# Reciprocals of the softmax sums turned by a transposing DMA instead of TensorE, and a pairwise minimum whose subtraction comes first

## The chip, the cores and the metric

The kernel runs on one core of a Trainium2 chip. The core has TensorE (PE; its weight loads are listed apart as PEld), VectorE (DVE), ScalarE (ACT) and GpSimd (POOL); each executes its own queue of instructions in order and waits at semaphores. SyncE (SP) issues nearly all of this kernel's DMAs, in order as well. SBUF is the on-chip memory, PSUM holds what PE writes, DRAM is off the core. The metric is the device time of one execution in microseconds (us), the median of some runs.

## The reference

```python
# q, k, v: (B, H, S, D) = (8, 8, 576, 64); w_in: (512, 2048); w_out: (2048, 512); all float32
scores = (1 / sqrt(D)) * q @ k.T                  # per batch and head, 576 x 576
kth = 32nd largest of each row
scores = where(scores >= kth, scores, -1e9)
attn = exp(scores - max(scores))
attn = attn / (sum(attn) + 1e-9)
x = (attn @ v) with heads side by side            # (4608, 512)
h = x @ w_in
out = (h * 1 / (1 + exp(-1.702 * h))) @ w_out     # (4608, 512)
```

## The kernel before, in words

**Slots.** Attention is cut into 144 slots. A slot is a batch, a tile of 128 query rows and a pair of heads; the last 64 rows of a batch are put together by two head pairs. A batch has 18 slots. The order of the work on each engine is written out by hand. Slots 0 to 12 are done one by one in an opening, in which the weights are loaded too. From slot 13 on a loop, `two_slots` (lines 852 to 942), handles two slots at a time, 68 passes in all. What follows is this loop; a pass is called a period.

**Scores and search.** PE multiplies q and k (line 283), ACT copies the 128 x 2 x 576 scores to SBUF (line 295). To find the 32nd largest of a row, DVE works on pairs of scores: `pair_up` (lines 319 to 328) writes the larger of each pair, `greater` (line 324, DVE), and the smaller, `lesser`. GpSimd makes the latter in 32-bit integer arithmetic on the bit patterns as a + b - max(a, b): the addition is line 327, the subtraction line 328. `topk_of_pairs` (lines 330 to 371) is a list of 23 DVE steps: fourteen MAX8 and MATCH_REPLACE8 on `greater` (numbers 0 to 13), then `pair_up` for the next slot (14), then six on `lesser` (15 to 20), and two reductions (21 and 22), the last of which writes `cut` (line 357). The function `find` (lines 868 to 874) executes the list and hangs other work between its steps.

**Softmax.** `lows` (line 378, GpSimd) makes a bias from `cut`; ACT pushes down what is below the cut (line 398), exponentiates and sums the rows (line 401). The sums of two slots stand together in `sums`, 128 x 4. `split` (line 471, ACT) puts the high and the low 16-bit halves of the exponentials apart and a DMA writes them to DRAM as `rows` (line 473); a transposing DMA, which handles 2-byte elements, reads them back turned, as `pt` (line 479).

**Values and x.** One period later PE multiplies `pt` and v into the PSUM tile `o` (`values_at`, line 539); the columns of `o` are query rows. Each is to be divided by its row's sum, which lies along partitions in `sums`. So `invert` (lines 425 to 437) adds 1e-9 (line 430) and takes reciprocals (line 432) on DVE, and GpSimd copies each to 64 columns (`wide`, line 434). It is called after step 8 of the odd slot's search, for the two slots of the period before. `sum_rows` (line 528) turns `wide` on PE against the identity matrix, twice a period, into the other half of `o`. Then ACT copies all of `o` to SBUF (`x`, line 924) and GpSimd multiplies the one half by the other (`x_of`, line 553) into `xT`. `finish_x` hands on an `xT` whose four head pairs are complete.

**Hidden layer.** `hidden` (line 587) multiplies `xT` and `w_in` in quarters, two quarters a period; ACT takes tanh (line 604) and copies (607), GpSimd forms the gated value (616, 617), PE multiplies by `w_out` (`project`, line 635), and ACT and a DMA take the result out (641, 643).

**Queues.** On PE a period is: a quarter of `hidden`, `project`, `sum_rows`, scores, values, scores, the second quarter of `hidden`, `project`. On GpSimd it is: lows and gate, lines 434 and 327 and 328, lows and gate, `x_of`, lines 327 and 328. SP issues: fetches of q and k in some periods (lines 185, 188), rows of the first slot, q and k split in halves in other periods (245 to 250), the transposing DMA of the first slot, of q and k (254), rows and transposing DMA of the second slot, v and out.

**Buffers.** The pool `raws` has eight buffers that are handed out in turn to `lesser`, `wide`, `x` and the copy `h` of the hidden layer; `lefts` has two, for `greater` and what the search leaves.

Of the kernel before, what the change touches and what calls it, by code (L numbers as in the profile page):

```python
# [9 lines left out]
ALU = mybir.AluOpType  # L10
ENG = mybir.EngineType
F32 = mybir.dt.float32
U32 = mybir.dt.uint32
I32 = mybir.dt.int32
U16 = mybir.dt.uint16
PSUM = bass.MemoryType.PSUM
DRAM = bass.MemoryType.DRAM

P = 128
# [11 lines left out]
def kernel(  # L31
# [27 lines left out]
    nc = tc.nc  # L59

    B, H, S, D = q.shape
# [29 lines left out]
    pool = lambda name, bufs, **kw: ctx.enter_context(tc.tile_pool(name=name, bufs=bufs, **kw))  # L91
    raws = pool("raws", 8)
# [6 lines left out]
    small = pool("small", 4)  # L99
# [3 lines left out]
    thp = pool("thp", 5)  # L103
    apart = pool("apart", 4, space=DRAM)
    apart_qk = pool("apart_qk", 2, space=DRAM)
    ps_s = pool("ps_s", 2, space=PSUM)
    ps_t = pool("ps_t", 2, space=PSUM)
    ps_h = pool("ps_h", 1, space=PSUM)
# [2 lines left out]
    ident = const.tile([P, P], F32, name="ident")  # L111
# [6 lines left out]
    raw = {}  # L118
# [198 lines left out]
    greater, lesser = {}, {}  # L317

    def pair_up(n):

        sc = st[n]["sc"]
        a, b = sc[:, :, 0:HALF], sc[:, :, HALF:S]
        greater[n] = lefts.tile([P, 2, HALF], F32, name="greater", tag="left")
        nc.vector.tensor_tensor(out=greater[n][:], in0=a, in1=b, op=ALU.max)  # L324
        lesser[n] = raws.tile([P, 2, HALF], F32, name="lesser", tag="raw")
        whole = lesser[n][:].bitcast(I32)
        nc.gpsimd.tensor_tensor(out=whole, in0=a.bitcast(I32), in1=b.bitcast(I32), op=ALU.add)  # L327
        nc.gpsimd.tensor_tensor(out=whole, in0=whole, in1=greater[n][:].bitcast(I32), op=ALU.subtract)  # L328

    def topk_of_pairs(n):  # L330

# [84 lines left out]
    sums = {}  # L416

    def sums_of(n):
# [3 lines left out]
            sums[k] = small.tile([P, 2, 2], F32, name="sums")  # L422
        return sums[k][:, n % 2, :]

    def invert(n):

        k = n // 2
        if k in sums:
            total = sums[k][:]
            nc.vector.tensor_scalar_add(total, total, 1e-9)  # L430
            inverse = small.tile([P, 4], F32, name="inverse")
            nc.vector.reciprocal(inverse[:], total.rearrange("p s j -> p (s j)"))
            wide = sums[k] = raws.tile([P, 2, 2, D], F32, name="wide", tag="raw")
            nc.gpsimd.tensor_copy(
                out=wide[:].rearrange("p s j d -> p (s j) d"),
                in_=inverse[:].unsqueeze(2).to_broadcast([P, 4, D]),
            )

    def turn(n, first, blocks):
        pr = st[n]["pr"]  # L440
# [42 lines left out]
    def x_at(b, t, hp):  # L483

        if t < NF:
            if (b, t) not in xts:
                xts[b, t] = xtp.tile([P, CC, P], F32, name="xT")
            return xts[b, t][:, hp, :]
        if b // 2 not in xts:
            xts[b // 2] = xtt.tile([P, CC, P], F32, name="xT_t")  # L490
        return xts[b // 2][:, hp, b % 2 * TAIL : (b % 2 + 1) * TAIL]
# [31 lines left out]
            put_off.append(bring)  # L523


    def sum_rows(m, to):

        nc.tensor.transpose(to, sums[m // 2][:, m % 2, :, :], ident[:])  # L528

    def values_at(m, o):  # L530

        b, t, hps = slots[m]
        pt = st[m]["pt"]
        for p in range(2 if t == NF else 1):
            cols = slice(p * TAIL, (p + 1) * TAIL) if t == NF else slice(0, P)
            main, tail = vv[b, hps[p]]
            for c in range(NF + 1):
                for j in range(2):
                    nc.tensor.matmul(  # L539
                        o[j * D : (j + 1) * D, cols],  # L540
                        lhsT=main[:, j, c, :] if c < NF else tail[:, j, :],
                        rhs=pt[:, MAIN[j] + c if c < NF else NF, cols],
                        start=(c == 0),
                        stop=(c == NF),
                    )
        st[m].clear()

    def x_of(m, o, by):

        b, t, hps = slots[m]  # L550
        for p in range(2 if t == NF else 1):
            cols = slice(p * TAIL, (p + 1) * TAIL) if t == NF else slice(0, P)
            nc.gpsimd.tensor_tensor(out=x_at(b, t, hps[p]), in0=o[:, cols], in1=by[:, cols], op=ALU.mult)
        finish_x(m)

    def finish_x(m):

        b, t, hps = slots[m]
        if hps[-1] < NP - 1:
            return  # L560
        if t == NF:
            if b % 2:
                first = [(b - 1 + i) * S + FULL for i in range(2)]
                rows = [(slice(i * TAIL, (i + 1) * TAIL), out[x : x + TAIL, :]) for i, x in enumerate(first)]
                xT = xts.pop(b // 2)
                ready.append(([xT[:, c, :] for c in range(CC)], [rows]))
            return
        lines = out[b * S : b * S + FULL, :].rearrange("(p t) c -> p t c", t=NF)
        xT = xts.pop((b, t))
        ready.append(([xT[:, c, :] for c in range(CC)], [[(slice(0, P), lines[:, t, :])]]))  # L570
# [80 lines left out]
    def leave_all():  # L651
        while leaving:
            leaving.pop(0)()
# [40 lines left out]
    def finish_one():  # L694
        unfinished.pop(0)()

    def may_project(waiting):

        return len(to_project) > waiting and len(finished) >= NG * CC + to_project[0][1].stop
# [62 lines left out]
    def bring_all():  # L762

        waiting = len(ready)
        while put_off:
            put_off.pop(0)()
        if len(ready) > waiting:
            hidden()
# [83 lines left out]
    def two_slots(n):  # L852

        first, second = [later.pop(m, []) for m in (n, n + 1)]
        live = lambda m: 0 <= m < N
        aside = n < N

        def begin(todo):
            for fn, args in todo:
                if fn is not prepare and fn is not prepare_by_dma:  # L860
                    fn(*args)

        def prepare_some(todo):
            for fn, args in todo:
                if fn is prepare or fn is prepare_by_dma:
                    fn(*args)

        def find(m):
            for i, op in enumerate(topk_of_pairs(m) if live(m) else [lambda: None] * 23):
                op()  # L870
                if i == 8 and m % 2:
                    invert(m - 2)
                if i > 1 and unfinished:
                    finish_one()

        def project_one():
            if may_project(0):
                project(True)

        def measure(m):  # L880
            if live(m):
                bounds(m)
            gate(aside)

        opens = n == SETTLED + 1
        begin(first)
        measure(n - 1)
        if opens:
            scores(n + 2)
            bring_all()  # L890
        if live(n - 1):
            exponentials(n - 1)
            split(n - 1)
        if opens:
            copy_scores(n + 2)
            tanh(aside)
        find(n)
        hidden(ps_t if opens else None)
        project_one()
        tanh(aside)  # L900
        prepare_some(first)
        held = [m for m in (n - 3, n - 2) if live(m) and "rows" in st[m]]
        o = ps_t.tile([P, 2, 2, P], F32, name="o", tag="tp") if held else None
        for i, m in enumerate(held):
            sum_rows(m, o[:, i, 0, :])
        if live(n + 2) and not opens:
            scores(n + 2)
            copy_scores(n + 2)
        leave_all()
        for i, m in enumerate(held):  # L910
            values_at(m, o[:, i, 1, :])
        if live(n - 1):
            turn_by_dma(n - 1)
        while turns:
            turns.pop(0)()
        if live(n + 3):
            scores(n + 3)
        begin(second)
        measure(n)
        def bring():  # L920
            if not held:
                return
            x = raws.tile([P, 2, 2, P], F32, name="x", tag="raw")
            nc.scalar.copy(out=x[:], in_=o[:])
            for i, m in enumerate(held):
                x_of(m, x[:, i, 1, :], x[:, i, 0, :])

        if live(n):
            exponentials(n, bring)
        else:  # L930
            bring()
        if live(n):
            split(n)
            turn_by_dma(n)
        hidden(ps_t)
        if live(n + 3):
            copy_scores(n + 3)
        tanh(aside)
        prepare_some(second)
        project_one()  # L940
        leave_all()
        find(n + 1)

    with tc.manual_schedule():
# [39 lines left out]
```

## Time and profile before

| | |
|---|---|
| median of three runs | 1482.66 us (1482.02 to 1483.18) |
| the profiled execution | 1482.51 us, its span 1480.7 us |
| instructions | 31436 |
| DMA | 242.20 MB, mean 164 GB/s |
| first and last `cut` of the paired search | 158.5 us and 1412.7 us of the span |
| one period of the loop | 19.1 us |

A group's row gives line, engine, operation, what it writes and reads, the shapes, the count, then busy time in us, the mean of one in ns, and the engine's idle time before them with what ended it. A row of the timeline gives start, duration, engine, line and operation, and in brackets the idle time of the engine before it. "SPq" is SP issuing DMAs. Times in the timeline are us from the start of the span. A time that an engine spends inside an instruction, waiting for memory ports included, is counted as busy.

### The profile page before, as it was taken

What the parts mean: (1) busy time and instruction counts of PE and PEld (TensorE: products, weight loads), DVE (VectorE), ACT (ScalarE), POOL (GpSimd) and SP (SyncE); (2) the same over time, 40 slices, a digit from 0 to 9 for tenths busy, and PEclk for the clock granted to TensorE, in tenths of its full rate; (3) what the DMA queues carried; (4) which work ended last, traced back from release to release, by engine and by line L of the source; (5) the groups of instructions that cost most, each with busy time, mean ns of one, the idle gap of its engine ahead of it and who ended that gap; (6) DMA issues with size and microseconds to landing.
All of it is one profiled execution on the core that took longest, in us unless ns stands there. A gap on an engine that the chain in (4) does not pass through costs nothing.

```text
span 1480.7 us, 31436 instructions
## 1 busy us (share of the span) xinstructions
PE 1442.7 (97%) x10784; PEld 1056.0 (71%) x10784; DVE 1382.9 (93%) x4541; ACT 1177.6 (80%) x1865; POOL 859.2 (58%) x1119
## 2 busy tenths in 40 slices
PE   7789899999999999999999999999999999999998
PEld 5667656777777777777777777777777777777776
DVE  7999989999999999999999999999999999999920
ACT  7998688878788887888878797888878798777730
POOL 3777545566655665666656556665565566665610
PEclk8899999999999999999999999999999999999999
DMA  8451256767667676776678686675767766545430
GB/s 245 135 156 51 72 159 180 202 172 179 173 181 201 159 196 179 178 189 178 170 180 200 168 193 171 183 195 163 179 175 203 174 187 184 140 131 132 127 87 15
DMA packets 516321, 242.20 MB, mean 164 GB/s; under 512 B 452672, under 2 KB 490560, under 8 KB 516160
## 3 DMA queue, kind: packets, MB, share of 16 engines
q1 hardware_dynamic: 515728, 239.89, 61.6%
q8 instruction: 85, 1.39, 0.4%
q14 instruction: 76, 0.62, 0.1%
q10 hardware_dynamic: 432, 0.30, 0.1%
HBM read 45.09 MB, written 102.24 MB: 99 GB/s over the span
## 4 chain that ended last, share of the span: by engine, by line
PE 88%; DVE 10%; ACT 2%; issue 0%; POOL 0%; POOLq 0%; ACTq 0%; DVEq 0%
PE ph L587 34%; PE po L635 32%; PE o L539 10%; PE s_ps L283 10%; DVE top L305 4%; DVE left L308 3%; PE o L528 1%; DVE top L345 1%; PE tp L449 1%; DVE wout L153 0%; DVE left L348 0%; PE none L170 0%; DVE greater L324 0%; ACT pr L401 0%; DVE win L153 0%
## 5 line engine op out<-in xcount | busy, mean ns | idle before, releaser
L635 PE MATMUL po<-wout,th 128*128 128x512 f32 x1152 | 518.6, 593 | 1.1 <-ACT ob L641 1.1
L587 PEld LDWEIGHTS ph<-xT,win 128*128 128x128 f32 x4096 | 472.1, 192 | 53.8 <-issue 52.2
L587 PE MATMUL ph<-xT,win 128*128 128x128 f32 x4096 | 484.4, 277 | 0.0
L635 PEld LDWEIGHTS po<-wout,th 128*128 128x128 f32 x1152 | 208.0, 190 | 211.0 <-issue 208.5
L345 DVE MAX8 top<-left 128x8 f32<-128x288 f32 x792 | 325.2, 445 | 0.0
L471 ACT COPY sc<-pr 128x2304 uint16<-128x2304 uint16 x132 | 278.8, 2112 | 4.2
L295 ACT ACTIVATE sc<-s_ps 128x576 f32<-128x576 f32 x288 | 170.9, 646 | 130.2 <-PE s_ps L283 130.2
L328 POOL TENSOR_TENSOR lesser<-lesser,greater 128x576 int32<-128x576 int32 x132 | 186.2, 1411 | 126.5 <-DVE greater L324 126.3
L348 DVE MATCH_REPLACE8 left<-top,left 128x288 f32<-128x288 f32 x528 | 229.6, 442 | 0.0
L401 ACT ACTIVATE pr<-sc,low 128x576 f32<-128x576 f32 x288 | 220.7, 772 | 0.0
L398 ACT ACTIVATE sc<-sc,cut 128x576 f32<-128x576 f32 x288 | 207.2, 772 | 12.4 <-DVE cut L357 5.8
L345 DVE MAX8 top<-lesser 128x8 f32<-128x288 f32 x528 | 213.5, 444 | 0.0
L327 POOL TENSOR_TENSOR lesser<-sc 128x576 int32<-128x576 int32 x132 | 187.0, 1417 | 2.4 <-ACT sc L295 2.4
L283 PE MATMUL s_ps<-qk_t 64*128 64x288 f32 (+1 forms) x1280 | 183.2, 433 | 0.3 <-ACT qk_t L219 0.3
L617 POOL TENSOR_TENSOR th<-th,h 128x512 f32<-128x512 f32 x128 | 163.7, 1279 | 10.7
L378 POOL TENSOR_SCALAR low<-cut,top 128x1 f32<-128x1 f32 x264 | 65.7, 265 | 175.6 <-DVE cut L357 174.1
L324 DVE TENSOR_TENSOR greater<-sc 128x576 f32<-128x576 f32 x132 | 153.8, 1165 | 11.7 <-ACT sc L295 5.5
L539 PE MATMUL o<-pt,v_l 128*64 128x128 f32 (+1 forms) x2368 | 144.4, 265 | 0.0
L539 PEld LDWEIGHTS o<-pt,v_l 128*64 128x64 f32 x2368 | 120.6, 138 | 25.7 <-issue 22.9
L604 ACT ACTIVATE th<-ph 128x512 f32<-128x512 f32 x144 | 85.9, 596 | 54.9 <-PE ph L587 48.3
L283 PEld LDWEIGHTS s_ps<-qk_t 64*128 64x128 f32 (+1 forms) x1280 | 99.4, 178 | 41.0 <-issue 23.1
L348 DVE MATCH_REPLACE8 left<-top,greater 128x288 f32<-128x288 f32 x264 | 114.7, 442 | 0.0
(86 smaller groups left out, 1535.7 us busy)
## 6 DMA issues: line engine op xcount, KB each, us to landing
rows<-sc SPq DMA_DIRECT2D x132, 576.0 KB, 3.2
qk_rows<-halves SPq DMA_DIRECT2D x48, 256.0 KB, 2.8
qk_l<-in_q_dram SPq DMA_DIRECT2D x64, 128.0 KB, 2.9
raw<-in_moe_w_in_dram SPq DMA_DIRECT2D x16, 512.0 KB, 4.9
v_l<-in_v_dram SPq DMA_DIRECT2D x32, 256.0 KB, 3.1
raw<-in_moe_w_out_dram SPq DMA_DIRECT2D x16, 512.0 KB, 3.5
out_dram<-ob SPq DMA_DIRECT2D x32, 256.0 KB, 2.9
qk_l<-in_k_dram SPq DMA_DIRECT2D x62, 128.0 KB, 2.9
```

Of the source, the lines that this page charges most:

```text
L283: nc.tensor.matmul(ps[i][rows, c, 0:HALF], lhsT=qT[b, hps[p]][on, cols], rhs=kT[b, hps[p]][on, FIRST[i] + c * HALF : FIRST[i] + (c + 1) * ...
L295: nc.scalar.mul(out=to, in_=ps[i][:, :, 0:HALF], mul=SCALE)
L327: nc.gpsimd.tensor_tensor(out=whole, in0=a.bitcast(I32), in1=b.bitcast(I32), op=ALU.add)
L328: nc.gpsimd.tensor_tensor(out=whole, in0=whole, in1=greater[n][:].bitcast(I32), op=ALU.subtract)
L345: nc.vector.max(found(r, i, True), src[:, i, :])
L348: nc.vector.match_replace(to[:, i, :], found(r, i), src[:, i, :], LOWEST)
L398: nc.scalar.activation(sc[:, i, :], sc[:, i, :], AF.Prelu, bias=cut[:, i : i + 1], alpha=HUGE)
L401: nc.scalar.activation(pr[:, i * S : (i + 1) * S], sc[:, i, :], AF.Exp, bias=low[:, i : i + 1], accum_out=den[:, i : i + 1],)
L471: nc.scalar.copy(out=halves, in_=pr[:].bitcast(U16).rearrange("p (k h) -> p h k", h=2))
L539: nc.tensor.matmul(o[j * D : (j + 1) * D, cols], lhsT=main[:, j, c, :] if c < NF else tail[:, j, :], rhs=pt[:, MAIN[j] + c if c < NF else ...
L587: nc.tensor.matmul(ph[:, i * tiles * P : (i + 1) * tiles * P], lhsT=win[:, c, f * P : (f + 1) * P], rhs=xT[c], start=(c == 0), stop=(c == ...
L635: nc.tensor.matmul(po[:], lhsT=gT[:, i * P : (i + 1) * P], rhs=wout[:, f, :], start=(f == 0), stop=(f == FC - 1))
```

## The change

The smaller of a pair is now formed as a - max(a, b) + b: the subtraction first, then the addition.

The reciprocals are no longer turned by PE. `invert` is called after step 16 of the even slot's search, in the period in which the sums were made, right behind the odd slot's exponentials. GpSimd writes the reciprocals to `wide` as 16-bit halves, high and low halves apart, each repeated 64 times, and a DMA on SP writes this to DRAM (`by_rows`, 128 KB). In the next period, after `values_at`, `turn_inverses` issues a transposing DMA on SP that reads it back as `by_t`: 128 x 128 x 2, the turned reciprocals of both slots, interleaved. `x_of` multiplies by every second column of it. `sum_rows` is gone, and `o` and `x` are half as wide.

```diff
-        nc.gpsimd.tensor_tensor(out=whole, in0=a.bitcast(I32), in1=b.bitcast(I32), op=ALU.add)
-        nc.gpsimd.tensor_tensor(out=whole, in0=whole, in1=greater[n][:].bitcast(I32), op=ALU.subtract)
+        nc.gpsimd.tensor_tensor(out=whole, in0=a.bitcast(I32), in1=greater[n][:].bitcast(I32), op=ALU.subtract)
+        nc.gpsimd.tensor_tensor(out=whole, in0=whole, in1=b.bitcast(I32), op=ALU.add)
...
+    inverses = {}
+
     def invert(n):
 
         k = n // 2
-        if k in sums:
-            total = sums[k][:]
-            nc.vector.tensor_scalar_add(total, total, 1e-9)
-            inverse = small.tile([P, 4], F32, name="inverse")
-            nc.vector.reciprocal(inverse[:], total.rearrange("p s j -> p (s j)"))
-            wide = sums[k] = raws.tile([P, 2, 2, D], F32, name="wide", tag="raw")
-            nc.gpsimd.tensor_copy(
-                out=wide[:].rearrange("p s j d -> p (s j) d"),
-                in_=inverse[:].unsqueeze(2).to_broadcast([P, 4, D]),
-            )
+        if k not in sums:
+            return
+        total = sums.pop(k)[:]
+        nc.vector.tensor_scalar_add(total, total, 1e-9)
+        inverse = small.tile([P, 4], F32, name="inverse")
+        nc.vector.reciprocal(inverse[:], total.rearrange("p s j -> p (s j)"))
+        wide = raws.tile([P, 2, 2, 2, D], U16, name="wide", tag="raw")
+        nc.gpsimd.tensor_copy(
+            out=wide[:],
+            in_=inverse[:].bitcast(U16).rearrange("p (s j h) -> p s h j", s=2, h=2).unsqueeze(4).to_broadcast([P, 2, 2, 2, D]),
+        )
+        rows = inverses[k] = apart_by.tile([P, 2, 2, P], U16, name="by_rows")
+        nc.sync.dma_start(rows[:], wide[:].rearrange("p s h j d -> p s h (j d)"))
+
+    def turn_inverses(n):
+
+        rows = inverses[n // 2]
+        by = inverses[n // 2] = raws.tile([P, P, 2], F32, name="by_t", tag="raw")
+        nc.sync.dma_start_transpose(
+            out=by[:].rearrange("p q s -> p (q s)").bitcast(U16), in_=rows[:].rearrange("q s h c -> (q s h) c")
+        )
...
-    def sum_rows(m, to):
-
-        nc.tensor.transpose(to, sums[m // 2][:, m % 2, :, :], ident[:])
...
-    def x_of(m, o, by):
+    def x_of(m, o):
 
         b, t, hps = slots[m]
+        by = inverses[m // 2][:, :, m % 2]
...
-                if i == 8 and m % 2:
-                    invert(m - 2)
+                if i == 16 and m % 2 == 0:
+                    invert(m - 1)
...
-        o = ps_t.tile([P, 2, 2, P], F32, name="o", tag="tp") if held else None
-        for i, m in enumerate(held):
-            sum_rows(m, o[:, i, 0, :])
+        o = ps_t.tile([P, 2, P], F32, name="o", tag="tp") if held else None
...
         for i, m in enumerate(held):
-            values_at(m, o[:, i, 1, :])
+            values_at(m, o[:, i, :])
+        if held:
+            turn_inverses(n - 2)
         if live(n - 1):
             turn_by_dma(n - 1)
...
-            x = raws.tile([P, 2, 2, P], F32, name="x", tag="raw")
+            x = raws.tile([P, 2, P], F32, name="x", tag="raw")
             nc.scalar.copy(out=x[:], in_=o[:])
             for i, m in enumerate(held):
-                x_of(m, x[:, i, 1, :], x[:, i, 0, :])
+                x_of(m, x[:, i, :])
```

More of the change, by code (lines that the diff above doesn't have):

```diff
@@ L105 @@
     apart_qk = pool("apart_qk", 2, space=DRAM)
+    apart_by = pool("apart_by", 2, space=DRAM)
     ps_s = pool("ps_s", 2, space=PSUM)
```

## The prediction

> **What bounds the kernel now.** I read the page's busy shares first, then the busy time inside the steady stretch (242 to 1400 us), then the groups by line, then the timeline of two periods of the paired loop, and last the single lines whose durations scatter. First the page's part 1, and below it the busy time by engine between 242 and 1400 us (columns: PE, weight loads, DVE, ACT, POOL, then clock, DMA share, GB/s), with the DVE time of line 324 alone in the same stretch:
>
> ```profile
> PE 1442.7 (97%) x10784; PEld 1056.0 (71%) x10784; DVE 1382.9 (93%) x4541; ACT 1177.6 (80%) x1865; POOL 859.2 (58%) x1119
> ...
> 242.00:1400.00 1158.00, 1158.00 (x8767) 843.31 (x8766) 1141.41 (x3880) 957.39 (x1452) 701.52 (x924) 1.00 0.68 176
> ...
> 242.00:1400.00 1158.00, 142.75 (x122) 1.00 0.68 176
> ```
>
> PE is busy for all of 1158.00 us at clock 1.00: it sets the pace, and the view of waits has nothing for PE in this stretch. But DVE is at 1141.41, nearly full too. How full it really is depends on line 324. Groups by line and shape (busy us, mean ns, then idle time before them):
>
> ```profile
> L528 PE MATMUL o<-ident,wide 128*128 128x128 f32 x132 | 25.3, 273 | 0.8 <-ACT qk_t L219 0.8
> L327 POOL TENSOR_TENSOR lesser<-sc 128x576 int32<-128x576 int32 x132 | 187.0, 1417 | 2.4 <-ACT sc L295 2.4
> L324 DVE TENSOR_TENSOR greater<-sc 128x576 f32<-128x576 f32 x132 | 153.8, 1165 | 11.7 <-ACT sc L295 5.5
> L434 POOL COPY wide<-inverse 128x256 f32<-128x256 f32 x66 | 26.2, 396 | 91.5 <-DVE inverse L432 91.5
> L924 ACT COPY x<-o 128x512 f32<-128x512 f32 x66 | 38.6, 585 | 6.5 <-PE o L539 6.5
> ```
>
> The timeline (start, duration) says why line 324 has a mean of 1165 ns:
>
> ```profile
> 806.02 0.88 POOL L553 TENSOR_TENSOR xT<-x 128x128 f32<-128x128 f32 x2 [1.48 <-ACT x L924]
> 806.86 1.41 POOL L327 TENSOR_TENSOR lesser<-sc 128x576 int32<-128x576 int32 x1
> 807.36 1.52 DVE L324 TENSOR_TENSOR greater<-sc 128x576 f32<-128x576 f32 x1
> ...
> 817.49 0.76 DVE L324 TENSOR_TENSOR greater<-sc 128x576 f32<-128x576 f32 x1
> 818.17 0.81 DVE L345 MAX8 top<-lesser 128x8 f32<-128x288 f32 x2
> 818.39 1.41 POOL L328 TENSOR_TENSOR lesser<-lesser,greater 128x576 int32<-128x576 int32 x1 [1.10 <-DVE greater L324]
> 818.90 0.07 DVE L348 MATCH_VALUE_LOAD lesser<-top,lesser 128x8 f32 x1
> ...
> 820.48 0.38 PE L528 MATMUL o<-ident,wide 128*128 128x128 f32 x2
> ...
> 820.79 1.24 PE L283 MATMUL s_ps<-qk_t 64*128 64x288 f32 x8
> ```
>
> With GpSimd idle the maximum takes 0.76 us. When it starts inside L327 it does not run until L327 ends (806.86+1.41 = 808.27) and finishes 0.61 later: a wait booked as busy time. This happens once in a period of two slots, 19.1 us long. So DVE has slack: 142.75 - 122 x 0.759 = 50.2 us over 1158/19.1 = 60.6 periods, 0.83 a period. DVE's own work is 19.1 - 0.83 = 18.27 a period. The MAX8 beside L328 are not slowed. Does a short one-input DVE operation wait in the same way? Duration min/median/max of three lines, and one moment of the opening:
>
> ```profile
> L324 DVE TENSOR_TENSOR greater<-sc x132: 737/759/1973, 144.8 to 1399.7; 128x576 f32<-128x576 f32 x132
> ...
> L409 DVE TENSOR_SCALAR some<-den x12: 144/150/1009, 23.8 to 150.3; 128x2 f32<-128x2 f32 x12
> ...
> L430 DVE TENSOR_SCALAR sums<-sums x66: 146/150/161, 179.9 to 1420.5; 128x4 f32<-128x4 f32 x66
> ...
> 150.02 1.28 POOL L145 TENSOR_TENSOR wout<-wout,raw 128x512 int32<-128x512 int32 x1
> ...
> 150.32 1.01 DVE L409 TENSOR_SCALAR some<-den 128x2 f32<-128x2 f32 x1 [2.26 <-ACT pr L401]
> ```
>
> L409, two elements wide, took 1.01 instead of 0.15 when it began inside a GpSimd operation, and ended 0.03 after it. The reciprocal right behind it took 0.17, as always.
>
> **The change part by part.** Durations are from the profiled execution: 1482.51 us, of which the span is 1480.7; the median of the runs is 1482.66, 0.15 above.
>
> *PE loses both transposes of the sums.* From L528's first product (820.48) to the next group (820.79) is 0.31 us; 66 pairs (L434 x66) make 20.5 us off the engine that sets the pace. PE's period falls to 18.8.
>
> *The maximum is no longer held.* The GpSimd subtraction now needs `greater`, so nothing of the pair runs beside it: DVE gets back 0.83 x 66 = 54.8 us. `lesser` is ready 1.4 us later than now after the maximum; its first reader comes a whole search (14 DVE operations, over 6 us) later, which hides it.
>
> *The inversion moves.* Line 430 (0.15) and the reciprocal (0.18) move from the odd slot's first search to the even slot, behind the two MAX8 that follow `pair_up`: no change of DVE's own work. But there GpSimd is now in the subtraction. From the rows at 817.49: it starts 0.90 after the maximum does and ends at 0.90+1.41 = 2.31; line 430 comes up at 1.41 (where 818.90 has the next operation), and would end at 1.56. Held as L409 was, it ends at 2.34: 0.79 lost, once a period. Lower bound 0 (L430's own row), upper bound the end of the addition behind it, 2.31+1.41 = 3.72, so 2.2. I take 0.79: L409 is the same operation, on fewer elements, and it got in at the first end of a GpSimd operation. The sums it needs (the last exponential's accumulator, 826.57 in the period where line 430 would come up at 826.40+1.41 = 827.81) are 1.2 us early.
>
> *DVE sum:* (0.79 - 0.83) x 66 = -2.6 us. Its period is 18.27+0.79 = 19.06, longer than PE's 18.8: DVE takes over, and nearly all of PE's 20.5 is not collected.
>
> L430's row, 161 ns at most, would put the move at nothing and the total at PE's -20.5. The Trainium skill, page "SBUF — State Buffer", section "Who interferes with whom", says of this what the row cannot: `tensor_scalar` may use the pair of ports that DVE shares with GpSimd, and whoever starts first holds it for the whole instruction, which by its rule gives about the -2.6 above.
>
> *GpSimd.* The wide copy writes 512 two-byte elements instead of 256 words: 0.40 becomes 0.62 if it goes as the 512-element tensor_scalar of line 616 does (617 ns); bounds 0.40 and 1.4. Subtract, add, copy end at 0.90+2.82+0.62 = 4.35 after the maximum; the next bounds wait for `cut`, which comes 2.78 after the maximum's end (820.84+0.19 against 818.25) plus 0.33+0.79 of inversion, 4.66. Hidden; without that cover up to 0.5 on a chain with 1.5 us to spare (lows end 812.27, first exponential 815.5).
>
> *ACT.* The copy of `o` is half as long, about 0.38 (between 0.27 for 128 and 0.59 for 512 elements): x is there 0.2 earlier. ACT is not a bound.
>
> *Two DMAs a period on SP.* The write (0.54 on SP, as the 576 KB rows) goes in front of the fetches of q and k; the transposing one stands in front of the slot's own. Each 576 KB transposition waits some 2.6 us on SP for its rows to land, so the new one fits that gap. `pt` is read over 5 us after it lands. What counts is when `by_t` lands, since `x_of` now waits for it, and behind `x_of` in GpSimd's queue stand the subtraction, the addition, the copy, the bounds and the gate. SP's queue in a period with six fetches, and the landing times of the 576 KB transposition:
>
> ```profile
> 305.84 0.59 SPq L473 DMA_DIRECT2D rows<-sc  x1
> 309.12 2.63 SPq L479 DMA_TRANSPOSE pt<-rows  x1
> ...
> DMA to landing us min/median/max: 4.2/4.6/6.5
> ```
>
> The new one is issued at 305.84+0.59+0.54 = 306.97. For 128 KB I take 2.9 us, the landing of a plain 128 KB DMA (bounds 2.1, a 32 KB one, and 4.6): 309.87. `x_of` began at 309.09 there and would now run from 309.9 to 310.8, across the maximum at 310.44: 0.2 lost on DVE. 28 periods have such fetches; in about half, when PE runs ahead, ACT and so SP come earlier: 14 x 0.2 = +2.9. In the 24 periods where q and k are written out, the issue is at 344.7, landing at 347.6, `x_of` ends at 348.5 just as the maximum starts: nothing. Also, in 16 periods PE's third and fourth hidden product need the xT just written. They have 0.24 to 0.43 us to spare now; 0.9 us later `x_of` makes PE wait about 0.7 in eight and 0.3 in the other eight, 8 us in all. PE has 20.5 to give, so this stays behind DVE.
>
> *End.* PE alone works from 1413 on; two pairs there give 0.6, and PE can end up about 1.0 ahead of where it stood against DVE. Sum: 1482.5 - 2.6 + 2.9 - 0.6 - 1.0 = 1481.
>
> **Rivals.** *PE stays the bound* (line 430 is not held, or slips in ahead of the subtraction because GpSimd is behind): DVE needs 18.3, PE 18.8: 1482.5 - 20.5 = 1462. For: L430's own row; against: L409. *The transposed inverses land late* (slower): if 128 KB take the 4.6 us of 576 KB, `by_t` lands at 311.6 and 349.3, and PE waits 2.4 and 2.0 us in the 16 periods: 35 us against 20.5, 1497. It decides from 1.3 us of wait per event, about 3.5 us from issue to landing. For: these DMAs are in queues that are busy 68%; against: the size. *Line 430 is held through both GpSimd operations*: +(2.2-0.83) x 66 = 90, 1573. Against: at 150 us DVE got in at the first end.
>
> **How the numbers follow.** DVE takes over: 0.50, 1481, own range 1474 to 1489 (hold 0.79 +-0.07, late `x_of` in none or all 28). PE stays the bound: 0.22. Late landing: 0.20, 1484 to 1500. Held through both: 0.05; rest 0.03. 0.2%, about 3 us, is what a measurement can tell from no change. Faster: 0.17 of the first and the second, 0.40 with a little of the rest; same: 0.21 from the first; slower: 0.39. The range 1461 to 1500 leaves out the 1573 and the tails.
>
> **What would show it.** Line 324 at 0.76 throughout; line 430 (new number) near 0.94; PE with idle time in the steady stretch, about 0.3 a period, waiting for DVE's products or xT; line 528 gone. Wrong, if line 430 stays at 0.15 with PE still full, or if GpSimd's wait before `xT` is for the transposing DMA by microseconds.

## The result and the profile after

The changed kernel takes **1499.57 us** (median of four runs, 1498.04 to 1503.33) against 1482.34 us for the kernel before (four runs, 1481.94 to 1483.18). The ratio is 1.0119, with a 95% interval of 1.0098 to 1.014: the change made the kernel slower by 17 us. 1481 had been forecast, with a range of 1461 to 1500. The profiled execution of the changed kernel has a span of 1498.7 us (1480.7 before) and a mean granted TensorE clock of 0.982.

Line numbers after: the subtraction of the pair is L328, the addition L329, the maximum L325, the addition of 1e-9 L434, the reciprocal L436, the wide copy L438, the write of `by_rows` L443, the transposing DMA of `by_t` L449, `rows` L487, the large transposing DMA L493, `x_of` L564, `values_at` L549, `hidden` L598, `project` L646, ACT's copy of `o` L935.

First the busy shares of the page, and below them the busy time by engine between 242 and 1400 us (PE, weight loads, DVE, ACT, POOL, clock, DMA share, GB/s):

```profile
PE 1440.9 (96%) x10652; PEld 1046.6 (70%) x10652; DVE 1352.4 (90%) x4541; ACT 1163.1 (78%) x1865; POOL 881.4 (59%) x1119
...
242.00:1400.00 1158.00, 1143.49 (x8497) 823.76 (x8496) 1098.21 (x3832) 932.57 (x1432) 712.24 (x910) 0.99 0.74 188
```

No engine took over. PE, which had been busy for all 1158.00 us, now idles 14.5; DVE, which should have become full, fell from 1141.41 to 1098.21; and the clock is 0.99 where it was 1.00. The view of waits names what the engines stood for (us in all, times, longest):

```profile
POOL xT L564 <- DMA by_t<-by_rows: 194.2, 38, 7.6
...
DVE sums L434 <- ACT pr L402: 46.2, 41, 5.8
POOL xT_t L564 <- DMA by_t<-by_rows: 38.3, 6, 7.8
...
PEld ph L598 <- POOL xT L564: 15.8, 13, 3.8
...
PE ph L598 <- POOL xT L564: 13.1, 7, 3.6
```

GpSimd stands 232.5 us in front of `x_of`, waiting for the new transposing DMA. Before, it stood there for ACT's copy, 100.0 us on line 553, and PE waited for nothing in the steady stretch. Now PE waits for `xT`, up to 3.6 us at a time. The timeline of one such moment:

```profile
313.47 0.63 SPq L189 DMA_DIRECT2D qk_l<-in_k_dram  x1
314.03 0.37 ACT L935 COPY x<-o 128x256 f32<-128x256 f32 x1
...
314.20 0.54 SPq L487 DMA_DIRECT2D rows<-sc  x1
...
314.78 1.50 SPq L449 DMA_TRANSPOSE by_t<-by_rows  x1
...
314.99 0.71 PE L598 MATMUL ph<-xT,win 128*128 128x128 f32 x4
...
318.54 0.88 POOL L564 TENSOR_TENSOR xT<-x,by_t 128x128 f32<-128x128 f32 x2 [7.25 <-DMA by_t<-by_rows]
...
319.05 6.01 PE L598 MATMUL ph<-xT,win 128*128 128x128 f32 x28 [3.35 <-POOL xT L564]
319.37 1.40 POOL L328 TENSOR_TENSOR lesser<-sc,greater 128x576 int32<-128x576 int32 x1
```

`x` is there at 314.40, but `by_t` was issued only at 314.78, behind six fetches and `rows`, and lands 3.6 us later. GpSimd has stood for 7.25 us, and PE's third hidden product for 3.35. Then comes something that the list of waits does not show. The 28 products from 319.05 take 6.01 us. In another period the same 28 took 3.58:

```profile
590.92 3.58 PE L598 MATMUL ph<-xT,win 128*128 128x128 f32 x28 [1.74 <-POOL xT L564]
```

The granted clock (third column from the right) of three stretches, each behind one wait of PE for `xT`, says why:

```profile
317.80:324.63 6.83, 5.58 (x26) 5.58 (x27) 6.76 (x25) 1.36 (x3) 4.67 (x7) 0.50 0.60 173
669.30:672.71 3.41, 3.23 (x15) 3.23 (x16) 3.34 (x14) 1.51 (x3) 3.33 (x5) 0.50 0.99 254
1017.50:1020.91 3.41, 3.41 (x17) 3.34 (x16) 3.41 (x14) 0.00 (x0) 3.33 (x5) 0.50 1.04 311
```

After 240 us, 13.65 us were run at half clock, which is 6.8 us of work lost. The kernel before has no half clock between 230.6 and 1479.9 us.

### The profile page after: what moved, and what is told of

Its sections match the earlier page's. It is cut to its first block, busy times and chain, and to the rows that moved or that the text cites. A ratio compares the mean times of both kernels' runs of the same rounds, so it can differ in the third digit from the quotient of the medians.

```text
span 1498.7 us, 31351 instructions
## 1 busy us (share of the span) xinstructions
PE 1440.9 (96%) x10652; PEld 1046.6 (70%) x10652; DVE 1352.4 (90%) x4541; ACT 1163.1 (78%) x1865; POOL 881.4 (59%) x1119
## 4 chain that ended last, share of the span: by engine, by line
PE 68%; DMA 2%; ACT 2%; SPq 1%; POOL 1%; issue 1%; POOLq 0%; ACTq 0%
PE ph L598 27%; PE po L646 26%; PE s_ps L284 7%; PE o L549 7%; DMA by_t<-by_rows 2%; ACT sc L399 1%; POOL xT L564 0%; ACT sc L296 0%; DMA rows<-sc 0%; ACT pr L402 0%; SPq L186 0%; SPq L493 0%; ACT sc L485 0%; POOL lesser L328 0%; POOL th L628 0%
## 5 line engine op out<-in xcount | busy, mean ns | idle before, releaser
L598 PEld LDWEIGHTS ph<-xT,win 128*128 128x128 f32 x4096 | 479.8, 194 | 71.2 <-issue 51.6
L646 PE MATMUL po<-wout,th 128*128 128x512 f32 x1152 | 519.1, 593 | 2.6 <-POOL th L628 1.6
L598 PE MATMUL ph<-xT,win 128*128 128x128 f32 x4096 | 496.0, 279 | 13.4 <-POOL xT L564 13.1
L646 PEld LDWEIGHTS po<-wout,th 128*128 128x128 f32 x1152 | 208.0, 190 | 213.0 <-issue 208.8
L346 DVE MAX8 top<-left 128x8 f32<-128x288 f32 x792 | 320.8, 446 | 0.0
L328 POOL TENSOR_TENSOR lesser<-sc,greater 128x576 int32<-128x576 int32 x132 | 186.4, 1412 | 147.1 <-DVE greater L325 147.1
L564 POOL TENSOR_TENSOR xT<-x,by_t 128x128 f32<-128x128 f32 x116 | 56.9, 512 | 263.0 <-DMA by_t<-by_rows 194.2
L329 POOL TENSOR_TENSOR lesser<-lesser,sc 128x576 int32<-128x576 int32 x132 | 186.2, 1411 | 10.3
L549 PE MATMUL o<-pt,v_l 128*64 128x128 f32 (+1 forms) x2368 | 145.2, 266 | 0.0
L549 PEld LDWEIGHTS o<-pt,v_l 128*64 128x64 f32 x2368 | 121.3, 138 | 26.9 <-issue 23.3
L325 DVE TENSOR_TENSOR greater<-sc 128x576 f32<-128x576 f32 x132 | 102.6, 777 | 15.1 <-ACT sc L296 15.0
```

The costliest lines, as they stand in the source:

```text
L328: nc.gpsimd.tensor_tensor(out=whole, in0=a.bitcast(I32), in1=greater[n][:].bitcast(I32), op=ALU.subtract)
L329: nc.gpsimd.tensor_tensor(out=whole, in0=whole, in1=b.bitcast(I32), op=ALU.add)
L346: nc.vector.max(found(r, i, True), src[:, i, :])
L549: nc.tensor.matmul(o[j * D : (j + 1) * D, cols], lhsT=main[:, j, c, :] if c < NF else tail[:, j, :], rhs=pt[:, MAIN[j] + c if c < NF else ...
L598: nc.tensor.matmul(ph[:, i * tiles * P : (i + 1) * tiles * P], lhsT=win[:, c, f * P : (f + 1) * P], rhs=xT[c], start=(c == 0), stop=(c == ...
L646: nc.tensor.matmul(po[:], lhsT=gT[:, i * P : (i + 1) * P], rhs=wout[:, f, :], start=(f == 0), stop=(f == FC - 1))
```

## The experiments

The theory after the result: `by_t` lands late because of its place in SP's queue, and everything lost follows from that (*late*). The rivals: DVE's held addition, L434, sets the pace (*held*); or GpSimd's own order does (*order*). The kernels were timed beside the kernel before in the same session; ratios are to that.

**Nobody reads the transposed inverses.** All DMAs stay; `x_of` multiplies by a piece of `wout` that has long been there, so the rows are not divided.

```diff
-        by = inverses[m // 2][:, :, m % 2]
+        by = wout[:, 0, 0 : 2 * P].rearrange("p (q s) -> p q s", s=2)[:, :, m % 2]
```

> Edit: x_of multiplies by a slice of the weights instead of the turned inverses, so the rows are left undivided and scaled by something else; every DMA, the GpSimd copy and DVE's inversion stay where the changed kernel has them, but nobody waits for the transposing DMA. Late landing: 1462 to 1483, with no half clock after 240 us. DMA traffic or SP's time: stays at 1495 to 1500. Holding at the port: stays near 1481, DVE's period 19.06, if it alone was the bound.

Measured: 1472.34 us, ratio 0.9932 (0.9917 to 0.9946); span 1470.6. The busy time between 242 and 1400 us:

```profile
242.00:1400.00 1158.00, 1158.00 (x8720) 835.83 (x8719) 1147.31 (x3929) 952.56 (x1465) 729.67 (x933) 1.00 0.76 192
```

and the addition (duration min/median/max in ns):

```profile
L434 DVE TENSOR_SCALAR sums<-sums x66: 170/868/1209, 181.9 to 1406.4; 128x4 f32<-128x4 f32 x66
```

Without the wait PE is full again at clock 1.00, and the change gains 10 us instead of losing 17. The two DMAs themselves cost PE nothing: they are all there, at 192 GB/s. And DVE, with the addition held to 0.87 us in the median, does not set the pace. So the wait for `by_t` is worth 27 us.

**The subtraction first, alone.** The kernel before with only the order of the two GpSimd operations changed.

```diff
-        nc.gpsimd.tensor_tensor(out=whole, in0=a.bitcast(I32), in1=b.bitcast(I32), op=ALU.add)
-        nc.gpsimd.tensor_tensor(out=whole, in0=whole, in1=greater[n][:].bitcast(I32), op=ALU.subtract)
+        nc.gpsimd.tensor_tensor(out=whole, in0=a.bitcast(I32), in1=greater[n][:].bitcast(I32), op=ALU.subtract)
+        nc.gpsimd.tensor_tensor(out=whole, in0=whole, in1=b.bitcast(I32), op=ALU.add)
```

> Edit: the kernel before with only the order of the pair's two GpSimd operations changed (subtraction first). The maximum is no longer held: line 324 at 0.74 to 0.76 us throughout, DVE with 50 us of waits instead. As PE keeps its transposes and was the bound, the time is within 3 us of before, 1479 to 1485. If DVE was the bound in truth: 1430 to 1470.

Measured: 1482.64 us, ratio 1.0005 (0.9996 to 1.0015). The maximum, and the busy time by engine:

```profile
L324 DVE TENSOR_TENSOR greater<-sc x132: 736/759/944, 143.1 to 1396.6; 128x576 f32<-128x576 f32 x132
```

```profile
242.00:1400.00 1158.00, 1157.83 (x8764) 842.95 (x8763) 1095.42 (x3885) 954.09 (x1451) 704.09 (x923) 1.00 0.69 176
```

The maximum no longer stands at the port, DVE is busy for 46 us less, and the time is the same: PE is full in both. What DVE gets back is slack.

**The transposing DMA earlier.** `turn_inverses` at the start of the period's first half, behind the fetches of q and k and ahead of `rows`.

```diff
+        held = [m for m in (n - 3, n - 2) if live(m) and "rows" in st[m]]
         begin(first)
+        if held:
+            turn_inverses(n - 2)
...
-        if held:
-            turn_inverses(n - 2)
```

> Edit: the transposing DMA of the inverses is issued at the start of the period, in front of the rows of the first slot and of q and k, and no longer behind them. Late landing (the changed kernel's GpSimd waits 232.5 us for by_t, PE then waits for xT and its clock is halved after waits of 2.4 us and more): the wait for by_t falls under 40 us, the clock stays at 1.00 after 240 us, and the time falls from 1499.6 to what DVE or PE allow, 1462 to 1483. Holding of the addition of 1e-9 at the shared port alone: the time stays within 4 us of the changed kernel's. DMA traffic (17 MB more, two more issues a period) whatever its place: also within 4 us of the changed kernel's.

Measured: 1543.07 us, ratio 1.0413 (1.0383 to 1.0444). No theory had this one slower: *late* had 1462 to 1483, the others no change within 4 us. (The shortest wait of the changed kernel that was followed by half clock is 2.12 us, not the 2.4 of the expectation.) The waits of SP's queue:

```profile
SPq L493 <- DMA rows<-sc: 310.5, 110, 4.9
SPq L449 <- DMA by_rows<-wide: 89.2, 42, 3.7
```

In periods without fetches of q and k nothing lies on SP between the write of `by_rows` and the DMA that reads it back:

```profile
730.84 0.42 SPq L443 DMA_DIRECT2D by_rows<-wide  x1
...
733.86 1.15 SPq L449 DMA_TRANSPOSE by_t<-by_rows  x1
735.05 0.58 SPq L487 DMA_DIRECT2D rows<-sc  x1
```

SP issues in order, so it stands for the landing, 89.2 us in all, and `rows` stand behind it until 735.05. What is turned from them, `pt`, then comes late too; PE waits for it, which it does in neither kernel of the study, and 34.1 us after 240 us are run at half clock:

```profile
PE o L549 <- DMA pt<-rows: 16.9, 16, 2.5
```

`by_t` itself gained nothing: GpSimd still waits 232.5 us for it (211.4 in `xT`, 21.1 in `xT_t`), though it lands 2.6 us after its issue in the median. The slack of SP shows in the time for which it stands before `rows` until ACT's `split` is done, that is, in how long it is ahead of its work. Before, after, and here:

```profile
SPq L473 <- ACT sc L471: 129.5, 64, 4.7
```

```profile
SPq L487 <- ACT sc L485: 76.6, 44, 4.7
```

```profile
SPq L487 <- ACT sc L485: 25.4, 14, 4.7
```

It is a rough measure: in the kernel in which nobody reads the inverses the same wait is 47.7 us, and that one is fast.

**The same, without the addition of 1e-9** (`nc.vector.tensor_scalar_add` in `invert` left out).

> Edit: as e1, and the addition of 1e-9 (the one DVE operation there that was seen to be held by GpSimd) is left out; the sums are at least 1, so the reciprocals are the same in float32. Late landing plus holding: DVE's period falls to 18.1, PE alone is the bound at 18.8, 1460 to 1466, and 8 us or more under e1 if e1 is bound by DVE. If holding costs nothing: equal to e1 within 3 us.

Measured: 1537.78 us, ratio 1.0374 (1.0337 to 1.0411): 5.3 us below the one with it, the intervals overlapping. The wait for `by_t` is still 182.4 us in `x_of`. With *late* unmended this could not separate the theories; the pair was put again below, without the wait.

**The out DMA off SP.** The suspicion was that a DMA of the results, waiting for ACT, holds up SP's queue.

```diff
-                    nc.sync.dma_start(to, ob[on, :])
+                    nc.scalar.dma_start(to, ob[on, :])
```

> Edit of the changed kernel: the output's DMAs are issued by ACT, right behind its own copy, instead of by SP, whose queue then never stands behind PE's last projection. If SP's queue position is what makes the transposed inverses late: GpSimd's wait for by_t falls from 232.5 us to under 120 us, and 1475 to 1490. If only the landing time of the transposing DMA itself counts (2.4 to 6.0 us): 1495 to 1500, and the wait unchanged within 30 us.

Measured: 1495.86 us, ratio 1.0087 (1.0071 to 1.0104), and 224.4 us of waits for `by_t` where there were 232.5; under 120 had been expected if this was the cause. It is at most a small part.

**The output projection ahead of the hidden products.** In the second half `project_one()` moves in front of `hidden(ps_t)`: PE has other work while `xT` is late. DMAs and GpSimd stay as they are.

```diff
+        project_one()
         hidden(ps_t)
...
-        project_one()
```

> Edit of the changed kernel: in the second half of a period PE does the projection before the hidden layer's quarter that needs the xT just written, so that PE has 3.4 us of other work while the transposed inverses land; SP's queue is untouched. If the loss is PE's own wait for xT with the half clock behind it: no half clock after 240 us and 1472 to 1478. If the loss comes through GpSimd (lesser, lows and gate queued behind its wait for by_t) or through SP: 1490 to 1500 as the changed kernel.

Measured: 1484.95 us, ratio 1.0017 (1.0008 to 1.0027). The waits of GpSimd and the busy time between 242 and 1390 us:

```profile
POOL xT L564 <- DMA by_t<-by_rows: 216.7, 42, 7.1
```

```profile
242.00:1390.00 1148.00, 1144.00 (x8563) 826.63 (x8563) 1114.52 (x3862) 934.74 (x1440) 712.61 (x917) 1.00 0.75 190
```

GpSimd waits as long as ever, but PE's waits shrink to 4.0 us and the half clock behind them is gone. The time lies between the two that were expected. So 14.6 of the 27 us came through PE's own wait for `xT` and its clock. The other 12 remain while GpSimd is late: from 1246 us on, where `x_of` waits for `by_t` only once, a period of this kernel takes 18.89 us, as in the kernel in which nobody reads the inverses, so the order of PE's work costs nothing by itself. By its queue they should come through what stands behind `x_of`: the subtraction, the copy, the bounds, the gate. That is argued; no run separates them.

**The transposing DMA where SP has room.** `turn_inverses` is issued right behind the large transposing DMA of the second half, some 5 us before `x_of` needs it; that DMA, and the out DMA, move behind `find`, which issues the write of `by_rows`.

```diff
-        if held:
-            turn_inverses(n - 2)
...
             split(n)
-            turn_by_dma(n)
...
         project_one()
-        leave_all()
         find(n + 1)
+        if live(n):
+            turn_by_dma(n)
+        if n // 2 in inverses:
+            turn_inverses(n)
+        leave_all()
```

> Edit of the changed kernel: the same DMAs in another order on SP. The write of the inverses goes between the second slot's rows and its transposing DMA, where SP waits for a landing in any case, and the transposing DMA of the inverses comes right behind that one, half a period earlier than in the changed kernel; the output's DMA goes behind both. Place in SP's queue as the cause: GpSimd's wait for by_t under 20 us, no half clock after 240 us, 1469 to 1476 like the kernel in which nobody reads by_t (1472.3). SP's load as the cause (two more issues, 1.7 us a period): 1490 or more.

Measured: **1473.30 us** (1472.47 to 1473.45), ratio 0.9936 (0.9921 to 0.995). SP's timeline, and the moment that answers to the one at 314 us above:

```profile
306.74 1.21 SPq L449 DMA_TRANSPOSE by_t<-by_rows  x1
...
318.36 0.38 SPq L443 DMA_DIRECT2D by_rows<-wide  x1
321.12 2.51 SPq L493 DMA_TRANSPOSE pt<-rows  x1
323.73 1.20 SPq L449 DMA_TRANSPOSE by_t<-by_rows  x1
```

```profile
311.43 0.88 POOL L564 TENSOR_TENSOR xT<-x,by_t 128x128 f32<-128x128 f32 x2 [1.49 <-ACT x L933]
...
311.93 3.84 PE L598 MATMUL ph<-xT,win 128*128 128x128 f32 x32
...
313.50 1.41 POOL L328 TENSOR_TENSOR lesser<-sc,greater 128x576 int32<-128x576 int32 x1 [1.19 <-DVE greater L325]
314.07 0.86 DVE L434 TENSOR_SCALAR sums<-sums 128x4 f32<-128x4 f32 x1
```

SP's wait for the landing of `rows` now covers the landing of `by_rows`, and `by_t` has 4.7 us from its issue at 306.74 to `x_of`. GpSimd waits for ACT's copy again, and the 32 products run at full clock in one go. With the division in it, it is as fast as the kernel in which nobody reads the inverses, and faster than both kernels of this study.

**The same without the addition of 1e-9.** This is the pair that tells *held* apart.

> Edit: as e7, and the addition of 1e-9 is left out (sums are at least 1, so the reciprocals are the same in float32). The row of line 434 where nobody reads by_t has a median of 868 ns, 0.7 us of them held. Holding as the bound that is left: 1462 to 1468, PE's 18.8 us a period. PE as the bound already: equal to e7 within 3 us.

Measured: 1473.24 us, ratio 0.9936 (0.9921 to 0.9951): no difference. The busy time between 242 and 1390 us:

```profile
242.00:1390.00 1148.00, 1147.07 (x8658) 827.61 (x8657) 1083.89 (x3829) 943.18 (x1452) 716.21 (x925) 1.00 0.77 192
```

DVE is busy 1083.89 of 1148.00 us here, 1136.96 with the addition; PE has no room in either. *Held* falls as a bound.

**The addition of the pair first, three times.** The two GpSimd lines are put back in the old order, the rest stays: in the changed kernel, in the one with the DMA in SP's gap, and in that one without the 1e-9.

> Edit of the changed kernel: the pair's addition first again, as before; the turn by DMA stays. If the changed order of the pair gave nothing in the changed kernel (late landing is all): 1496 to 1503. If DVE is near its bound, as the sum of the prediction had it: the maximum is held 0.83 us and line 434 0.79 us a period, DVE needs 19.9 us a period, and the time is 1530 to 1550.

Measured: 1505.17 us, ratio 1.0149 (1.0128 to 1.0171), 5.6 above the changed kernel, the intervals just overlapping; 1496 to 1503 had been expected if the order gives nothing. Its profiled execution has three stretches of 6.83 us at half clock after 240 us, 20.5 us against the 13.65 of the changed kernel. What the new order may be worth there is small beside the 27 us of the wait.

> Edit of e7 (DMAs in SP's gap): the pair's addition first again. With both holds DVE needs 18.27 + 0.83 + 0.79 = 19.9 us a period against PE's 18.9: 1525 to 1545. If holds only take up slack that DVE has anyway: 1473, as e7.

Measured: 1475.34 us, ratio 0.9957 (0.994 to 0.9974): a clear miss for the sum in which both holds add up (1525 to 1545), while the other expectation, that holds only take up slack, had 1473. One moment of it, and the row of GpSimd's addition:

```profile
803.28 0.77 DVE L325 TENSOR_TENSOR greater<-sc 128x576 f32<-128x576 f32 x1
...
803.39 1.93 POOL L328 TENSOR_TENSOR lesser<-sc 128x576 int32<-128x576 int32 x1
...
804.70 0.65 DVE L434 TENSOR_SCALAR sums<-sums 128x4 f32<-128x4 f32 x1
...
L328 POOL TENSOR_TENSOR lesser<-sc x132: 1402/1412/1932, 140.3 to 1391.8; 128x576 int32<-128x576 int32 x132
```

The maximum started first, took its 0.77 us, and it was GpSimd's addition that took 1.93 instead of 1.41. But only 19 of the 121 additions between 242 and 1390 us took more than 1.5 us; in the other periods the pair hardly meets. In the kernel before, 60 of the 120 maxima of the stretch were held, one in every period. PE is busy for 1147.60 of the 1148.00 us, so neither hold costs time. Why the engines came to stand so against each other is not shown.

> Edit of e10, and the addition of 1e-9 is left out (sums are at least 1, so the reciprocals are the same in float32). Only the hold of the maximum is left: DVE 18.27 - 0.15 + 0.83 = 18.95 us a period, 1474 to 1482. The distance to e10 is then the price of the hold of line 434, 0.79 x 66 = 52 us by the prediction's figure if e10 is bound by DVE, and nothing if it is not.

Measured: 1471.64 us, ratio 0.9928 (0.9909 to 0.9947), 3.7 below the last one with intervals that overlap, and below the 1474 to 1482 expected. The tens of microseconds that the hold of line 434 would cost if DVE were the bound are not there.

## Why the prediction was wrong

**PE sets the pace, and loses work: right, but mis-sized.** The transposes are gone and nothing else of PE grew much, yet in the kernel with the DMA in SP's gap a period of full PE is 18.89 us (60 periods between ACT's copies of `o` at 254.26 and 1387.93), against 19.11 before: 0.22 saved, not 0.31. From the start of `project` ahead of the scores to the next group it is now 3.53 us where it was 3.44; why is not shown. The 66 pairs are worth about 14 us, and that kernel ends 10.0 us of span below the one before; it was 3.4 us behind at ACT's third copy of `o` (235.32 against 231.96), in the first periods of the loop.

**The maximum is no longer held: right.** Its median is 740 ns in the changed kernel, and the kernel with the order alone shows 759 with a maximum of 944. There it brings nothing by itself, 1482.64 us, as PE is full.

**Line 430 is held once, about 0.79: right where the order of the engines is as assumed.** It took 0.87 in the median with the DMA out of the way. In the changed kernel the median is 171 ns, since DVE mostly stood for ACT's sums or came when GpSimd was late:

```profile
L434 DVE TENSOR_SCALAR sums<-sums x66: 145/171/1424, 181.5 to 1434.5; 128x4 f32<-128x4 f32 x66
```

The rule of the Trainium skill that was weighed, page "SBUF — State Buffer", section "Who interferes with whom", agrees with 0.87 against 0.15, and with the 1.93 us of GpSimd where the maximum came first: it says that the one that issues first keeps the shared ports. What the hold costs the kernel is nothing that could be measured here, 1473.30 us with the addition and 1473.24 without.

**DVE takes over as the bound, period 19.06: this step failed.** DVE's own work was taken as the period less what the maximum lost, 18.27 us, which booked every small gap of DVE as work. The prediction's own row had it smaller: (1141.41 - 50.2)/60.6 = 18.0. The kernel without the addition has 1083.89/1148.00 x 18.89 = 17.84 us of it a period; with 0.15 for the addition and 0.79 for the hold that is 18.78, just below PE's 18.89. Only at the end of the changed kernel, where `by_t` was in time, did periods come out near the 19.06 forecast, with the addition at 1.06 to 1.07 us. The first maximum of each period there:

```profile
1274.43 0.74 DVE L325 TENSOR_TENSOR greater<-sc 128x576 f32<-128x576 f32 x1
...
1293.42 0.74 DVE L325 TENSOR_TENSOR greater<-sc 128x576 f32<-128x576 f32 x1
...
1312.53 0.74 DVE L325 TENSOR_TENSOR greater<-sc 128x576 f32<-128x576 f32 x1
```

**The new DMA fits SP's gap and lands at 309.87: this is the step that decided, and it failed.** Three terms were off. Its landing was taken as 2.9 us; it was 3.3 in the median and 6.0 at most. Its own time on SP, by which all that stands behind it moves, was not counted; it is 1.44 us in the median, beside the 0.53 of the write, which was counted:

```profile
L449 SPq DMA_TRANSPOSE by_t<-by_rows x66: 1142/1444/2895, 192.7 to 1445.3; - x66
...
DMA to landing us min/median/max: 2.4/3.3/6.0
```

And the issue time was taken from the old timeline, as if SP would stay where it was against PE. Before, `rows` were issued at 305.84, and PE's hidden products of that period began at 309.39, 3.6 us later; after, `rows` were issued at 314.20 and the products began at 314.99, 0.8 us later. The row of before, beside the 305.84 in the prediction:

```profile
309.39 3.84 PE L587 MATMUL ph<-xT,win 128*128 128x128 f32 x32
```

SP comes later against PE in the fast kernels too: 311.30 and 311.89 where nobody reads the inverses, and its wait ahead of `rows`, 129.5 us before, is 52.2 us in the kernel with the DMA in SP's gap. What differs is whether a DMA that `x_of` needs at once stands behind `rows`.

**The rival "the transposed inverses land late" decided.** Its price was 1497 by waits of 2.4 and 2.0 us in 16 periods. That it is near the 1499.57 is luck, since it is made up differently: PE idles 14.5 us in the steady stretch, less than the 35 forecast, but half clock, for which the prediction had no term, takes 6.8 more, and the saving to set against them is 14 us, not 20. Between the spans of this kernel and the one in which nobody reads the inverses lie 28.1 us: 14.5 and 6.8 make 21.3 of them. Of the remaining 6.8, 1.4 are there at ACT's fourth copy of `o` already (255.7 us against 254.3), before PE's first wait of the steady stretch; the other 5 are 0.2 to 0.5 us in each of some 16 periods, and not told apart.

**The copies on GpSimd and ACT: right.** The wide copy takes 0.61 us (0.62 forecast), ACT's copy 0.37 (0.38).

**The sign that was named as proving it wrong**, GpSimd's wait ahead of `xT` for the transposing DMA by microseconds, is the first line of the waits above.

## What to carry to other kernels

A DMA is costed like an instruction: by what stands ahead of it in its queue, by the time it occupies that queue, by its landing, and by what the consumer's queue holds behind the waiting instruction. A timeline of before gives its issue time only if the issuing queue keeps its slack; a queue that stands for its own inputs has slack, and this wait is one thing to watch, together with what stands in the queue behind it and how soon that is needed. An earlier place in the program is not an earlier place in time when the DMA must itself wait in line for a landing: put it behind a wait that is there anyway. An engine's hold on a port is a cost only beyond that engine's slack, and small gaps are not work.

## What the runs showed of the hardware

*Short waits halve TensorE's clock, and their length alone does not decide.* In the changed kernel a wait of 1.74 us ahead of the products left the clock at full, and so did shorter ones; waits of 2.12, 3.35 and 3.65 us were followed by 3.41, 6.83 and 3.41 us at half clock. The Trainium skill, page "TensorE: Matmul & The Clock Gate", section "Why this matters for your kernels", advises against idle gaps of more than about 3 us; the wait of 2.12 us at 669 us of this trace was enough, so the measurement decides. In other runs 1.95 us were enough (first row below, the out DMA off SP: 28 products in 5.03 us), and 3.12 us were not (second row and the clock behind it, the addition first in the changed kernel):

```profile
589.22 5.03 PE L598 MATMUL ph<-xT,win 128*128 128x128 f32 x28 [1.95 <-POOL xT L564]
...
669.43 3.59 PE L598 MATMUL ph<-xT,win 128*128 128x128 f32 x28 [3.12 <-POOL xT L564]
...
669.43:673.00 3.57, 3.57 (x29) 3.44 (x30) 3.57 (x14) 0.35 (x1) 3.49 (x4) 1.00 1.02 265
```

What fits is a fixed grid. The stretches at half clock begin whole multiples of 3.413 us apart; in the changed kernel they begin at 317.75, 669.32 and 1017.48 us, 103 and 102 steps apart. PE's idle time between 240 and 1395 us of the thirteen traces, laid on the grid of its trace, separates without exception: each of the 23 steps at full clock with 1.85 us of idle time or more is followed by a step at half clock, and none of the 4330 others, with 1.79 us at most, is. The 3.12 us fell into two steps, 1.73 and 1.39. At half clock, 10 steps with 0.84 us of idle time or more were followed by another at half clock, and 24 with 0.43 us or less by full clock. Between 20 and 240 us two steps do not fit (1.74 us with half clock behind it, 1.90 without), so the limit is roughly 1.8 us in a step, read from these traces only. A wait of PE here cost up to 3.4 us beyond its own length, half of 6.83.

*Which of two engines waits at the shared port is set by who starts first*: the same pair of operations cost DVE 0.83 us a period before; in the loop with the DMA in SP's gap and the addition first it cost GpSimd 0.52 us (1.93 less 1.41) in 19 of about 61 periods.

*A transposing DMA of 128 KB keeps SP for 1.14 to 2.90 us*, and how long it takes to land depends on its place: 3.3 us in the median of the changed kernel, 2.8 with the DMA in SP's gap, 2.6 at the start of the period.
